# A two-dimensional FFT beside a dense branch: spectral stage on fused real-complex matrices, weight loads on a second queue

## The chip, the cores and the metric

One core of one Trainium2 chip. The metric is the device time of one execution in microseconds (us). TensorE is called PE in the profile (PEld is its weight load), VectorE DVE, ScalarE ACT, GpSimd POOL, SyncE SP. For one core, the record calls a run "fast" when it is within 1.5% of the fastest run of the same kernel; that rule matters below, because it removes most runs of one kernel and few of the other.

## The reference

```python
def _A_ref(x, w_r, w_i):                       # x: (1, 2048, 512), w_r and w_i: (2048, 257)
    X = rfft2(x.astype(float32))
    X = X * (w_r + 1j * w_i)
    return irfft2(X, s=(2048, 512)).astype(bfloat16)

def _B_ref(x, w1, b1, w2):                     # 512 -> 1792 -> 512
    h = x @ w1 + b1
    sp = log1p(exp(-abs(h))) + where(h > 0, h, 0)
    return (h * tanh(sp)) @ w2

g = sigmoid((x * gate_w).sum(-1, keepdims=True))
return g * _A_ref(x, ...) + (1 - g) * _B_ref(x, ...)
```

Everything is bf16 on input. The two branches share only x and the last line, so their matmuls can be mixed freely.

## The kernel before

A Python list scheduler gives every engine a fixed order. It knows an assumed duration and a priority of each task, and it takes, among the tasks that could start within a tolerance of the earliest one, the one of highest priority:

```python
        EPS = 0.25          # tolerance
        SYNC_LAT = 0.25     # assumed latency from engine to engine
        ...
                if est <= best_est + EPS:
                    ...
                    elif (t.prio, t.bl, -t.idx) > (best[1].prio, best[1].bl, -best[1].idx):
                        best = (est, t)
```

The FFT is done by matmuls. Along the rows: `a1`, 16 matmuls of 256 columns for each of 16 row tiles, on half of the array's columns each (`ps<-fdgd,xT` in the profile), then a first stage along the sequence, `s1`. Its results go to a staging buffer of two halves, `T2` (also called `Y1s`; `T` in the profile). From there they are written to DRAM and read back in another order:

```python
            def f_e2(e, t=t, sbank=sbank):        # on ACT or DVE
                return e.activation(Y1s[(t // 4) % 2][:, (t % 4)::4, :], ps[:, sbank, :]..., AF.Copy)
            ...
            if t % 4 == 3:                        # after every fourth tile: two writes of 256 KB
                gi = t // 4
                for bx in range(2):
                    b0 = 16 * bx + 4 * gi
                    t_r1w.append(dma(f"r1w{gi}_{bx}", scr1_w[:, b0:b0 + 4, :], Y1s[gi % 2][:, 4 * bx:4 * bx + 4, :], ...))
```

The third group of four tiles therefore waits until the writes of the first have landed. After the read-back comes the stage that the change rewrites. Its real and imaginary parts lie on separate columns, so that a complex product takes four matmuls each way and an addition:

```python
            def f_s2(e, g=g, xbank=xbank):                      # PE, 4 x 256 columns
                px = ps[:, xbank, :].rearrange("p (c k) -> p c k", c=2)
                e.matmul(px[:, 0, :], CC, In2[:, g, 0, :], start=True, stop=False)
                e.matmul(px[:, 0, :], nSS, In2[:, g, 1, :], start=False, stop=True)
                e.matmul(px[:, 1, :], SSm, In2[:, g, 0, :], start=True, stop=False)
                return e.matmul(px[:, 1, :], CC, In2[:, g, 1, :], start=False, stop=True)
            ...   # DVE: Ps = px * Wr
            ...   # DVE: Qs = px (parts swapped) * WiT
            def f_wmz(e, g=g, pi=pi, zi=zi):                    # POOL
                return e.tensor_tensor(out=Zs[zi], in0=Ps[pi], in1=Qs[pi], op=ALU.add)
            ...   # POOL: column 0 of Zs replaced
            ...   # PE: four matmuls of 256 columns on Zs (s2i), then back through DRAM and s1i, a1i
```

The dense branch: `ps<-xT,w_sb` (mm1), evictions to `hsreg`, exp, ln and tanh on ACT, a product on POOL, `ps<-w_sb,hsreg` (mm2).

## Time and profile before

| what | us |
|---|---|
| median of 4 runs given at first | 171.28 (170.35 to 171.88) |
| median of 16 runs, beside the changed kernel | 171.30 (169.11 to 171.92) |
| the profiled run, its span | 171.84, 170.1 |
| PE busy in it | 159.5 |

The prediction shows the busy table, the chain and the groups. Two readings it did not show matter later. The first is the DMA row of the 40 slices (4.25 us each; a digit is the busy share in tenths):

```profile
DMA  5999999140258466000203020494022010101101
```

The loads fill the queue up to slice 7, 30 us. The second is the start of the timeline: start, duration, engine, operation, operands, count, and in brackets what was waited for.

```profile
4.52 1.92 PE L127 MATMUL ps<-fdgd,xT 128*64 128x256 bf16 x16 [0.96 <-DMA fdgd<-c_fd]
...
8.40 1.92 PE L127 MATMUL ps<-fdgd,xT 128*64 128x256 bf16 x16
...
11.64 1.60 PE L127 MATMUL ps<-fdgd,xT 128*64 128x256 bf16 x16
...
15.18 1.06 PE L127 MATMUL ps<-fdgd,xT 128*64 128x256 bf16 x16
```

The same sixteen matmuls take 1.92 us, then 1.60, then 1.06: the engine starts at about half its speed, and in this run it is at full speed only after 12 to 13 us. I read that row too late: it was in the profile before the prediction, which speaks of "some 14 us of start in which the loads pace PE".

### The profile page before, as it was taken

How to read it: one execution, taken by the hardware profiler on the slowest of the kernel's cores; microseconds unless marked ns; L12 is line 12 of the kernel's file. 1: busy time of each engine (PE TensorE's matmuls, PEld its weight loads, DVE VectorE, ACT ScalarE, POOL GpSimd, SP SyncE). 2: the span in 40 equal slices, each digit the busy share in tenths (PEclk: the TensorE clock that was granted, in tenths of full speed). 3: DMA queues.
4: the chain of work that ended last, by engine and by line, in shares of the span. 5: the costliest groups of instructions: out<-in, count | busy, mean ns of one | idle time of the engine just before them, and what ended most of it. 6: DMA issues, size and time to landing. Idle time of an engine off the chain costs nothing.

```text
span 170.1 us, 2886 instructions
## 1 busy us (share of the span) xinstructions
PE 159.5 (94%) x1130; PEld 88.5 (52%) x1130; DVE 99.2 (58%) x170; ACT 119.2 (70%) x89; POOL 91.0 (53%) x93
## 2 busy tenths in 40 slices
PE   1798999999999998999999999999999999999990
PEld 0576754557656334556666655445555554444440
DVE  1125431247875759978885887557787816071533
ACT  3124576789989997999899989999999980300000
POOL 1000009900000698999999999639991099940000
PEclk9999999999999999999999999999999999999999
DMA  5999999140258466000203020494022010101101
GB/s 166 279 400 390 409 384 339 33 123 4 74 175 233 140 210 285 0 0 31 98 10 118 29 94 39 156 303 122 0 86 99 4 66 0 62 17 49 62 0 62
DMA packets 15058, 21.90 MB, mean 129 GB/s; under 512 B 708, under 2 KB 11972, under 8 KB 14276
## 3 DMA queue, kind: packets, MB, share of 16 engines
q1 hardware_dynamic: 15044, 21.71, 37.7%
q8 instruction: 9, 0.15, 0.3%
q14 instruction: 5, 0.04, 0.1%
HBM read 15.41 MB, written 6.29 MB: 128 GB/s over the span
## 4 chain that ended last, share of the span: by engine, by line
PE 82%; DMA 11%; DVE 3%; issue 1%; SPq 1%
PE ps L127 82%; DMA scr<-T 5%; DMA hsreg<-in_A_x_dram 3%; DMA Abuf<-scr 3%; DVE bs L127 2%; DVE xT L127 1%; SPq L127 1%; DVE T L127 0%; SPq L864 0%; DVE hsreg L127 0%
## 5 line engine op out<-in xcount | busy, mean ns | idle before, releaser
L127 POOL TENSOR_TENSOR hsreg<-hsreg,ureg 128x896 bf16<-128x896 bf16 x32 | 59.4, 1879 | 34.3 <-ACT ureg L127 34.3
L127 PE MATMUL ps<-xT,w_sb 128*128 128x512 bf16 x224 | 53.9, 379 | 0.0
L127 PE MATMUL ps<-w_sb,hsreg 128*128 128x512 bf16 x224 | 51.9, 379 | 0.0
L127 ACT ACTIVATE ureg<-ureg 128x3584 bf16<-128x3584 bf16 x16 | 51.0, 3189 | 0.2
L127 PEld LDWEIGHTS ps<-w_sb,hsreg 128*128 128x128 bf16 x224 | 21.5, 98 | 24.6 <-POOL hsreg L127 0.5
L127 PEld LDWEIGHTS ps<-xT,w_sb 128*128 128x128 bf16 x224 | 20.7, 98 | 22.8 <-DVE hsreg L127 2.5
L127 DVE TENSOR_SCALAR hsreg<-ps,b1f 128x512 bf16<-128x512 f32 x31 | 22.9, 748 | 8.8 <-PE ps L127 7.6
L127 ACT ACTIVATE ureg<-hsreg 128x3584 bf16<-128x3584 bf16 x8 | 25.5, 3189 | 0.2
L127 DVE CAST T<-ps 128x512 bf16<-128x512 f32 x22 | 14.9, 689 | 15.5 <-PE ps L127 15.4
L127 DVE TENSOR_SCALAR bs<-ps,omg 128x512 bf16<-128x512 f32 x15 | 11.3, 751 | 21.5 <-PE ps L127 21.5
L127 ACT ACTIVATE hsreg<-ps,b1f 128x512 bf16<-128x512 f32 x25 | 17.1, 685 | 5.6 <-PE ps L127 5.5
L127 POOL TENSOR_SCALAR WiT<-wizp 128x4096 bf16<-128x4096 bf16 x2 | 7.2, 3604 | 24.1 <-DMA wizp<-in_A_w_i_dram 24.1
L127 PE MATMUL ps<-fdgd,xT 128*64 128x256 bf16 x256 | 18.9, 299 | 1.0 <-DMA fdgd<-c_fd 1.0
L127 POOL TENSOR_TENSOR wizp<-wizp 128x512 bf16<-128x512 bf16 x16 | 18.1, 1154 | 0.0
L127 PEld LDWEIGHTS ps<-fdgd,xT 128*64 128x64 bf16 x256 | 14.4, 120 | 5.0 <-issue 2.9
L127 PE MATMUL ps<-fdgd,TT 128*128 128x512 bf16 x64 | 15.6, 379 | 0.0
L127 DVE COPY xT<-ps 128x512 bf16<-128x512 bf16 x14 | 5.8, 423 | 14.7 <-PE ps L127 14.7
L127 ACT ACTIVATE Abuf<-ps 128x512 bf16<-128x512 f32 x9 | 5.4, 597 | 12.4 <-PE ps L127 12.4
L127 DVE SCALAR_TENSOR_TENSOR bs<-ps,gcol,bs 128x512 bf16<-128x512 f32 x16 | 12.0, 749 | 0.7 <-PE ps L127 0.3
L127 ACT ACT_TABLE_LOAD x9 | 11.5, 1283 | 0.9 <-PEq L929 0.8
L127 DVE TENSOR_TENSOR wizp<-ps,Wr_sb 128x512 bf16<-128x512 f32 x16 | 10.9, 684 | 0.4 <-PE ps L127 0.2
L127 DVE CAST TT<-ps 128x256 bf16<-128x256 f32 x24 | 9.0, 441 | 3.7 <-PE ps L127 3.7
(53 smaller groups left out, 107.3 us busy)
## 6 DMA issues: line engine op xcount, KB each, us to landing
w_sb<-in_B_w_dram SPq DMA_DIRECT2D x4, 896.0 KB, 14.6
scr<-T SPq DMA_DIRECT2D x8, 256.0 KB, 5.5
Abuf<-scr SPq DMA_DIRECT2D x2, 1024.0 KB, 6.2
scr<-T SPq DMA_DIRECT2D x4, 512.0 KB, 2.6
Abuf<-scr SPq DMA_DIRECT2D x4, 512.0 KB, 6.0
out_dram<-bs SPq DMA_DIRECT2D x8, 256.0 KB, 2.0
hsreg<-in_A_x_dram SPq DMA_DIRECT2D x3, 512.0 KB, 7.7
Wr_sb<-in_A_w_r_dram SPq DMA_DIRECT2D x1, 1028.0 KB, 15.1
```

The source lines that it names most:

```text
L127: return f(*a, **kw)
```

## The change

The intent is to put real and imaginary parts both on partitions, so that one 128x128 matrix does the whole complex rotation on 512 columns. The two products with the weights need not be added: two matrices sum them in PSUM. For that the weights must lie twice on the partitions, so they are loaded twice, on a second queue, issued from POOL. The diff cut to its core (`...` marks cuts):

```diff
 def _q_of(c, e):
-    return 32 * (e // 16) + 2 * (e % 16) + c
+    return 64 * c + e
...
-    small = np.stack([np.eye(128), CC, SS, -SS, P0, P1], axis=1)
+    small = np.stack([RF, RI1, RI2, P0k, P1k, Jm], axis=1)
...
+SCH = dict(eps=0.1, sync=0.1)
...
-        EPS = 0.25
-        SYNC_LAT = 0.25
+        EPS = SCH['eps']
+        SYNC_LAT = SCH['sync']
...
+NWARM = 0
+KN = dict(mm1c0=97.0, mm1c=94.0, mish=88.0, mul=89.0, mm2=70.0, bev=94.0, sp0=95.0, gate=96.5)
...
-        t_wr = dma("ld_wr", Wr_sb[:], Wrv, writes=["Wr"], nbytes=128 * 8224)
-        t_wi = dma("ld_wi", Wi_sb, Wiv, writes=["wizp"], nbytes=128 * 8224)
+        t_wr = dma("ld_wr", WaT..., Wrv, writes=["WaT"], nbytes=128 * 16448, queue="pool", deps=t_w1)
+        t_wi = dma("ld_wi", WbT..., Wiv, writes=["WbT"], nbytes=128 * 16448, queue="pool", deps=t_w1)
...          # the two loads of the second dense weights:
-                            writes=[("w2", h)], nbytes=128 * 7 * 1024, ndesc=896))
+                            writes=[("w2", h)], nbytes=128 * 7 * 1024, ndesc=896, queue="pool", deps=t_w1))
...
-        G.cur_prio = 75.0
+        G.cur_prio = KN['gate']
...          # making the negated copy of the imaginary weights (wit) removed; in its place
+        G.add("wb_sgn", "pool", ..., lambda e: e.tensor_scalar(out=WbT[:, :, :], in0=WbT[:, :, :], scalar1=sgnf[:, 0:1], ...))
...          # inside the loop of 16 steps:
-                px = ps[:, xbank, :].rearrange("p (c k) -> p c k", c=2)
-                e.matmul(px[:, 0, :], CC, In2[:, g, 0, :], start=True, stop=False)
-                ...three more
+                return e.matmul(ps[:, xbank, :], RFm, In2ck[:, 2 * gp:2 * gp + 2, :]..., start=True, stop=True)
...
-                return e.tensor_tensor(out=Zs[zi], in0=Ps[pi], in1=Qs[pi], op=ALU.add)
...
-                e.matmul(pt[:, 0, :], CC, Zs[zi][:, 0, :], start=True, stop=False)
-                ...three more
+                e.matmul(ps[:, tbank, :], RI1m, P1s[pi]..., start=True, stop=False)
+                return e.matmul(ps[:, tbank, :], RI2m, P2s[pi]..., start=False, stop=True)
```

The correction of column zero is rewritten to the new layout, with one more tiny matmul (`Jm`), and two scalings of the gate move from DVE to ACT. `NWARM` is a set of warm-up matmuls that is coded but switched off.

> **What bounds the kernel now.** I read the page first: the busy table, then the chain that ended last, because a busy engine only matters if the chain runs over it.
>
> ```profile
> PE 159.5 (94%) x1130; PEld 88.5 (52%) x1130; DVE 99.2 (58%) x170; ACT 119.2 (70%) x89; POOL 91.0 (53%) x93
> ...
> PE 82%; DMA 11%; DVE 3%; issue 1%; SPq 1%
> ```
>
> The tensor engine is 94% busy and carries 82% of the chain. Next, the same chain in order of time, for where it leaves the tensor engine.
>
> ```profile
> 17.09 32.44 PE ps L127 x304
> ...
> 51.41 8.48 DMA scr<-T
> ...
> 60.03 4.91 DMA Abuf<-scr
> 64.95 0.05 issue
> 64.99 99.49 PE ps L127 x576
> 164.48 0.02 issue
> ```
>
> The reader should see two things. From 64.99 to 164.48 us the chain is one unbroken stretch of matmuls. And the excursion through DRAM (51.4 to 65 us), although the chain names it, costs the engine nearly nothing. The table of waits and the busy times by stretch say so:
>
> ```profile
> PE ps L127 <- DMA Abuf<-scr: 0.7, 1, 0.7
> ...
> 2.96:17.09 14.13, 11.56 (x118) 8.64 (x119) 4.54 (x13) 3.58 (x6) 0.00 (x0) 1.00 0.99 353
> 17.09:65.00 47.91, 46.98 (x430) 26.09 (x430) 26.02 (x41) 41.35 (x34) 16.65 (x17) 1.00 0.60 199
> 65.00:104.00 39.00, 39.00 (x250) 23.98 (x251) 32.26 (x55) 36.21 (x29) 38.87 (x53) 1.00 0.15 59
> ```
>
> PE idles 0.7 us for the read-back, and 47.91 - 46.98 = 0.93 us in all from 17.09 to 65; the matmuls of the dense branch fill the rest. From 65 to 104 us, where the changed stage lies, PE is busy all 39.00 us. POOL is then busy 38.87 us, so there are two full engines in that stretch, and I must decide which one sets the pace. PE has no gap at all, so POOL does not make it wait. So the time is: 3.0 us until the first matmul, some 14 us of start in which the loads pace PE, 149 us of full PE, and a tail of about 4.1 us (two evictions and the last store after the last matmul ends at 165.97).
>
> The engine's real price is not the busy column. The matmul rows show 379 ns for one of 512 columns, but that is latency; they overlap. From the timeline a run of 28 takes 6.21 us, so the spacing is (6.21 - 0.379) / 27 = 0.216 us. A run of eight with 256 columns takes 1.04 us: (1.04 - 0.273) / 7 = 0.110 us.
>
> ```profile
> 145.74 6.21 PE L127 MATMUL ps<-w_sb,hsreg 128*128 128x512 bf16 x28
> ...
> 71.89 1.04 PE L127 MATMUL ps<-Abuf,sm 128*128 128x256 bf16 x8
> ```
>
> The groups concerned, with the shapes kept apart:
>
> ```profile
> L127 POOL TENSOR_TENSOR wizp<-wizp 128x512 bf16<-128x512 bf16 x16 | 18.1, 1154 | 0.0
> ...
> L127 PE MATMUL ps<-Abuf,sm 128*128 128x256 bf16 x64 | 9.0, 273 | 0.7 <-DMA Abuf<-scr 0.7
> L127 PE MATMUL ps<-wizp,sm 128*128 128x256 bf16 x64 | 8.5, 273 | 0.0
> ...
> L127 POOL TENSOR_SCALAR WiT<-wizp 128x4096 bf16<-128x4096 bf16 x2 | 7.2, 3604 | 24.1 <-DMA wizp<-in_A_w_i_dram 24.1
> ```
>
> Their busy times (9.0 and 8.5) contain overlap with neighbours of other groups at each change, so I price them by spacing: 64 x 0.110 = 7.0 us each.
>
> **What the Trainium skill says.** "TensorE: Matmul & The Clock Gate", section "Back-to-back issue gap", gives N / 2.4 + 2.5 ns for a warm array: 216 ns at 512 columns, 109 at 256. The trace agrees (0.216 and 0.110). The same section also names 131 ns per matmul at 512 for a sustained stream; this trace does not show that. The consequence is that cost goes by columns: one matmul of 512 columns saves almost nothing over two of 256, only fewer total columns do. "DMA: Bandwidth & Descriptors", section "Issuing engines are not separate DMA queues", says that transfers started by different engines still run on the same 16 DMA engines, so a second queue saves issue time[...], not bandwidth. Nothing in this trace tests it, since all data transfers are issued from SP; but the page shows DMA full (nines) only in the first seven slices. The same page, section "SWDGE vs HWDGE vs iDMA", says that GpSimd computes the descriptors itself and that the engines take turns between the two kinds of queue; no row here has a duration for that.
>
> **The change, part by part.**
>
> 1. Forward second stage. Before: 16 steps of four 256-column matmuls (real and imaginary parts on separate columns), 1024 columns a step. After: real and imaginary parts both lie on partitions, the whole complex rotation is one 128x128 matrix, one 512-column matmul a step. Cost: 64 x 0.110 = 7.0 us becomes 16 x 0.216 = 3.5 us. Saved: 3.5 us, all of it on PE in the full stretch.
>
> 2. Inverse second stage. Before: four of 256 columns a step, after the multiply and add. After: two of 512, since the two products go to PSUM unadded and two matrices sum them. Cost: 7.0 us becomes 32 x 0.216 = 6.9 us. Saved: 0.1 us. The gain goes to POOL instead.
>
> 3. POOL. The 16 additions leave: 18.1 us. Making the negated and copied imaginary weights (7.2 us) leaves, and the sign multiply over 8224 columns takes its place. At 3604 / 4096 = 0.88 ns a column that is an estimated 7.2 us, so nothing is won there. 16 small column patches stay. POOL loses about 18 us net, beside PE, and by the stretch above PE did not wait for it: 0 us on the path. Its value is that the products of the dense branch, which shared POOL with the additions (products and additions alternate from 65 to 102 us), come earlier. That gives the scheduler more matmuls to choose from.
>
> 4. DVE. Two products a step over 512 columns before and after (16 x 0.684 + 16 x 0.682 = 21.8 us): unchanged.
>
> 5. Weights. Both spectral weight tensors are read twice into duplicated partitions: 1.03 MB each becomes 2.1 MB, so 2.1 MB more. At the 390 to 400 GB/s of the full slices that is an estimated 5.3 us more of DMA. These loads now start from POOL after the dense first weights have landed, so roughly from 20 to 38 us with the second dense weights behind them (6 MB at 400 GB/s is 15 us). They are needed at 65 us (spectral) and 58 us (second dense layer): hidden.
>
> 6. The correction of column zero: four tiny matmuls become one, one swap matmul is added. I put -0.1 us on PE. Its chain gains one hop over PE and one over DVE. Two DVE scalings of the gate move to ACT: nothing.
>
> 7. The schedule. The order on every engine comes from a list scheduler. Its tolerance goes from 0.25 to 0.1 us, its assumed latency between engines also from 0.25 to 0.1, and the gate's matmuls move earlier. That removes no work. The small gaps inside full PE: after 17.09 us I count 146.3 us of matmuls by spacing in 147.9 us, so 1.6 us of them exist to be won. But a shorter assumed latency is optimistic: a matmul's result comes 379 - 216 = 163 ns after its slot is over, so a consumer placed 0.1 us later is placed too early. Taken together I book zero, with an uncertainty of 1 us either way.
>
> Sum on the path: 3.5 + 0.1 + 0.1 = 3.7 us, with perhaps 0.3 us from a shortened 0.7 us wait and a smoother tail. 171.28 - 4.0 = 167.3 us, a ratio of 0.977.
>
> **Rivals.**
>
> ACT becomes the bound. It is busy 35.26 of 35.5 us from 104 to 139.5 us, so it paces the dense branch. But its last large activation ends at 139.51 us, the last POOL product at 150.66; with one half group (7 x 0.216 = 1.5 us) and the tail of 4.1 us this limit is 156.3 us against a span of 170.1. A saving of 4 us does not reach it. If it did, the time would stay above 169.
>
> The new two-deep buffer stalls PE. The summed spectra had four buffers; the new products have two, and a step cannot go on until the inverse matmuls two steps before are done. These wait for the column-zero chain, with its two extra hops and POOL's products of 1.88 us in its way. PE issues in order, so a step placed too early holds everything behind it. Before, column zero was ready at about 75 us, ten after the read-back, and PE filled the time with other matmuls. For the rival: the optimistic latency of part 7. Against it: plenty of dense matmuls are left at that moment, and POOL is freer. I give it a loss of 0.5 to 2 us if it comes, so 168 to 169.5.
>
> The second queue disturbs the forward spectra. The writes to DRAM from 22 to 50 us, formerly behind the weights in one queue, now take turns with 6 MB of loads. If the two staging buffers fill, PE stops in order. It would cost 1 to 3 us, and 169 to 170. Against it: each staging buffer has over 10 us before it is needed again. It could even help, as the writes no longer stand behind weights.
>
> The reordering gains more than the matrices. If the scheduler recovers the micro gaps (1.6 us), part of the start and some of the tail, the time is 164 to 165.5.
>
> **Range and chances.** The removed columns are the certain part. The rest is roughly symmetric with a spread of about 2 us: 164.8 to 169.8 holds it 8 times in 10. The 2% line lies at 171.28 x 0.98 = 167.85, only half a microsecond above my number, so the chance of faster is only moderately above one half: 0.58. Slower needs a real stall of over 7 us somewhere, 0.04; the rest is 0.38.
>
> **What would show it right or wrong.** Right: the forward matmuls appear as 16 of 512 columns and the inverse as 32, PE has about 4 us less busy time, it is still 94% busy, POOL's busy time is some 18 us lower, and no new PE wait exceeds 1 us. DVE within 1 us of 99. Wrong in part 1: PE's busy time falls by 4 us and the span does not; then a new wait should stand between 20 and 50 us (staging, second queue) or between 65 and 105 us (column zero, two buffers). Wrong in part 7: the span falls by clearly more than PE's busy time, with the difference in the first 17 us or after the last matmul. Wrong in part 5: a wait for the weight loads ahead of the first spectral product, or the second dense layer starting well after 58.5 us.

## The result, and the profile after

| | median us | lowest to highest | runs |
|---|---|---|---|
| before | 171.30 | 169.11 to 171.92 | 16 |
| after | 169.49 | 166.61 to 171.30 | 11 |

The ratio of the fast runs is 0.9816, with an interval from 0.975 to 0.9883: the 2% line lies inside it, so the verdict is unclear. This ratio, and each below, is the mean time of one kernel's fast runs over that of the other's of the same rounds, so not quite the ratio of the medians quoted. Here the difference is large. Only 3 of the 11 runs after (166.61, 168.03, 168.16) are within 1.5% of the fastest, but 11 of the 16 before. Over all runs the means are 169.31 and 171.09, a ratio of 0.990. (The record's list of states has a twelfth run of after, 169.11 us, which its count leaves out; it would not change the reading.) So the first thing to explain is not a time but a spread: 4.7 us after, against 2.8 before.

The profile of after is of its fastest run (166.61 us), that of before is of one of its slower (171.84). A comparison of the two flatters the change: the spans differ by 5.3 us, the medians by 1.8. With that in mind, the page of after:

```profile
PE 155.6 (94%) x1047; PEld 77.8 (47%) x1047; DVE 100.5 (61%) x170; ACT 118.0 (72%) x90; POOL 78.0 (47%) x79
...
DMA  5999389994445859000030303038801113010101
...
PE 91%; DVE 3%; DMA 3%; issue 1%; SPq 0%
```

PE is 94% busy as before, with 3.9 us less of it, and the chain is PE even more than before. The DMA row has a dip in its fifth slice (a slice is 4.12 us here), and the loads then go on to the ninth, about 37 us. That is the second queue: its loads wait for the first dense weights to land. The groups of the new stage, and the stretches of the middle:

```profile
L144 PE MATMUL ps<-Abuf,sm 128*128 128x512 bf16 x16 | 4.9, 379 | 0.0
...
L144 PE MATMUL ps<-bs,sm 128*128 128x512 bf16 x32 | 8.4, 379 | 0.0
...
L144 POOL TENSOR_SCALAR WbT<-WbT,sgnf 128x8224 bf16<-128x8224 bf16 x1 | 7.1, 7118 | 0.1
```

```profile
15.64:53.60 37.96, 37.81 (x374) 21.03 (x374) 20.91 (x34) 31.02 (x30) 14.59 (x21) 1.00 0.68 241
53.60:104.00 50.40, 50.36 (x232) 21.44 (x233) 41.02 (x67) 48.45 (x30) 32.94 (x35) 1.00 0.28 102
```

The matmul counts are those of the diff, 16 and 32 of 512 columns. PE (first pair of each row) is busy 37.81 of 37.96 us and 50.36 of 50.40: nothing in the new stage makes it wait. POOL, which was full from 65 to 104 us, is now busy 32.94 of 50.4.

To separate the 5.3 us, I priced each matmul of both traces by its slot: columns / 2.4 ns + 2.5 ns (the formula of the prediction), the half-array `a1` ones 62 ns each, the tiny ones 27 ns (64 of the gate take 1.74 us). Together they come to 153.0 us before and 149.3 after, 3.7 less. The tail, from the last matmul's end to the span's end, is 4.14 and 4.11 us. The rest is the start, where after is ahead by 1.45 us and has done one more `a1` group, 1.0 us:

```profile
4.76 1.92 PE L144 MATMUL ps<-fdgd,xT 128*64 128x256 bf16 x16 [1.16 <-DMA fdgd<-c_fd]
...
8.04 1.21 PE L144 MATMUL ps<-fdgd,xT 128*64 128x256 bf16 x16
...
9.96 1.07 PE L144 MATMUL ps<-fdgd,xT 128*64 128x256 bf16 x16
```

Here the engine is almost at full speed in the second group and at full speed from the third; before, in its slower run, from the fourth. Against that, the time after the start (from 17.09 us before, 15.64 after) that no slot explains grew from 2.6 to 3.5 us, 0.85 more. Most of that is one row:

```profile
20.48 13.01 PE L144 MATMUL ps<-xT,w_sb 128*128 128x512 bf16 x56
```

(13.01 - 0.379) / 55 = 0.230 us a matmul where 0.216 would do. The new schedule issues the first chunk of the dense branch in one piece, and its two PSUM banks are emptied by DVE or ACT in between: weight loads waiting for an eviction by DVE rose from 2.5 to 8.2 us. The sum, 3.7 + 1.45 + 1.0 + 0.03 - 0.85 = 5.3 us, is what was to be explained, and 2.4 of it are the start.

The theories that I took to the experiments are three. **The matrices** take 3.7 us off, whatever else happens. **The start** at half speed differs from run to run and makes both kernels' times spread. **The second queue** (called theory C in some of the expectations) holds up the first write of the staging buffer in some runs of the changed kernel and stops PE; the rival is that the changed kernel's slow runs are nothing but slow starts.

On the start the Trainium skill has this: "TensorE: Matmul & The Clock Gate", section "What's actually happening", says that the array's clock is halved by default, that about 3.4 us of activity in a free-running window releases it, and that the moment therefore varies from run to run. The traces agree: 1.92 us against 1.06 for the same work. Their records of the granted clock, which the views do not list, begin with the release: at 8.39 us in after, 12.78 in before. (For the time ahead of that the views print 1.00 for want of a record, so the durations are the evidence there.)

### The profile page after: what moved, and what is told of

Its sections match the earlier page's. It is cut to its first block, busy times and chain, and to the rows that moved or that the text cites. A ratio compares the mean times of both kernels' runs of the same rounds, so it can differ in the third digit from the quotient of the medians.

```text
span 164.8 us, 2686 instructions
## 1 busy us (share of the span) xinstructions
PE 155.6 (94%) x1047; PEld 77.8 (47%) x1047; DVE 100.5 (61%) x170; ACT 118.0 (72%) x90; POOL 78.0 (47%) x79
## 4 chain that ended last, share of the span: by engine, by line
PE 91%; DVE 3%; DMA 3%; issue 1%; SPq 0%
PE ps L144 91%; DMA hsreg<-in_A_x_dram 3%; DVE bs L144 2%; DVE xT L144 1%; SPq L144 0%; DVE hsreg L144 0%; DVE T L144 0%
## 5 line engine op out<-in xcount | busy, mean ns | idle before, releaser
L144 DVE TENSOR_SCALAR hsreg<-ps,b1f 128x512 bf16<-128x512 f32 x37 | 27.7, 750 | 14.6 <-PE ps L144 13.4
L144 PEld LDWEIGHTS ps<-xT,w_sb 128*128 128x128 bf16 x224 | 19.1, 97 | 30.0 <-DVE hsreg L144 8.2
L144 PE MATMUL ps<-fdgd,xT 128*64 128x256 bf16 x256 | 17.9, 286 | 1.2 <-DMA fdgd<-c_fd 1.2
L144 DVE CAST T<-ps 128x512 bf16<-128x512 f32 x19 | 12.8, 687 | 6.6 <-PE ps L144 6.4
L144 PEld LDWEIGHTS ps<-fdgd,xT 128*64 128x64 bf16 x256 | 13.6, 114 | 4.1 <-DVE xT L144 1.8
L144 ACT ACTIVATE hsreg<-ps,b1f 128x512 bf16<-128x512 f32 x19 | 13.0, 684 | 3.4 <-PE ps L144 3.2
L144 DVE TENSOR_TENSOR bs<-ps,WaT 128x512 bf16<-128x512 f32 x16 | 10.3, 684 | 0.3 <-PE ps L144 0.3
L144 DVE TENSOR_TENSOR bs<-ps,WbT 128x512 bf16<-128x512 f32 x16 | 10.2, 682 | 0.0
L144 DVE CAST TT<-ps 128x256 bf16<-128x256 f32 x22 | 8.1, 438 | 3.0 <-PE ps L144 3.0
L144 POOL DMA_DIRECT2D WaT<-in_A_w_r_dram x1 | 0.8, 803 | 19.0 <-DMA w_sb<-in_B_w_dram 19.0
```

The costliest lines, as they stand in the source:

```text
L144: return f(*a, **kw)
```

## The experiments

Three sets of runs, on three chips; kernels of one set ran on the same chip and are compared there. "Warm" below means that a few matmuls on zeros are put ahead of the first work and between the first two pieces of it, so that the clock is released earlier (in the two profiles of experiment 2, at 5.27 us before and 6.93 after).

### 1. The changed kernel again, nothing edited

> The changed kernel once more, unedited, for a second profile. The first profiled run (166.61 us) was the fastest of 11, the kernel before was profiled in one of its slower runs (171.84). Theory A (the tensor engine's start at half clock lasts differently long from run to run): in a run near the median of 169.5 us, the first groups of 16 forward matmuls take about 1.9 us instead of 1.06 for longer than in the first profile (where only the first did), and the stretch after 17 us is as long as in the first profile within 0.3 us. Rival B (a wait in the middle that comes and goes, from the second queue or the two buffers): the start is as in the first profile and a new wait of the tensor engine of 1 to 3 us stands after 17 us.

Median 166.96 us of 8 runs (166.37 to 170.92), before on the same chip 170.26 of 43 (169.08 to 172.69), ratio 0.9803 (0.9756 to 0.9849). Six runs lie between 166.37 and 168.70, and two are at 169.45 and 170.92. By luck the profiled run is the one of 169.45, 2.8 us slower than the profiled run of after. Theory A expected no longer stretch after 17 us and rival B no slower start; each is half right, for its start shows one slow group more (the clock is released at 10.44 us):

```profile
7.98 1.92 PE L144 MATMUL ps<-fdgd,xT 128*64 128x256 bf16 x16
...
10.87 1.06 PE L144 MATMUL ps<-fdgd,xT 128*64 128x256 bf16 x16
```

And later it has this, in the order of time, from its timeline:

```profile
20.57 0.80 POOL L144 DMA_DIRECT2D WaT<-in_A_w_r_dram  x1 [19.18 <-DMA w_sb<-in_B_w_dram]
...
21.29 0.92 SPq L144 DMA_DIRECT2D scr<-T  x2
...
41.43 0.60 ACT L144 ACTIVATE T<-ps 128x512 bf16<-128x512 f32 x1 [2.57 <-DMA scr<-T]
...
42.17 0.38 PE L144 MATMUL ps<-Abuf,m1g 128*128 128x256 bf16 x2 [2.00 <-ACT T L144]
```

The same lines of the fastest run (after):

```profile
20.36 0.80 POOL L144 DMA_DIRECT2D WaT<-in_A_w_r_dram  x1 [18.98 <-DMA w_sb<-in_B_w_dram]
...
20.38 0.92 SPq L144 DMA_DIRECT2D scr<-T  x2
...
38.55 0.60 ACT L144 ACTIVATE T<-ps 128x512 bf16<-128x512 f32 x1 [0.60 <-DMA scr<-T]
```

Read them from the bottom. The eviction into staging waits until the first pair of writes has left the buffer. In the fast run that costs ACT 0.60 us and PE nothing. In the slow run the pair was issued 0.91 us later, after POOL's first load instead of level with it. The two writes of the pair have to be told apart here. In the fast run the first landed 2.2 us after its issue and only the second was held up, for 17.7 us, to 38.44. In the slow run both were, for 17.0 and 19.6 us, and the second landed at 41.32 (the median of the twelve writes is 2.6 us in both runs). ACT then waits 2.57 us and PE 2.00. So the slow run has both causes at once: some 0.9 us from the start, 2.0 from the staging buffer. The two are linked: a slow start delays the write, while the loads are tied to the landing of the first dense weights and don't move with it.

Both queues share the engines. In the fast run between 18 and 46 us:

```profile
q0 software_dynamic: 768, 6.05, 56.3%
q1 hardware_dynamic: 2139, 1.08, 12.8%
```

The columns are packets, MB, and the share of the engines. POOL's queue moves packets of 7.9 KB on average, 16,448 B for the spectral weights; the writes are packets of 0.5 KB.

### 2. Both kernels warm

```diff
-NWARM = 0
+NWARM = 4                     # four 512-column matmuls on zeros before the first transposes
...
+            if t == 0:          # and two more after the first tile's transposes
+                G.add("warm2", "pe", 2 * 0.43, f_warm2, reads=["wreg", ("x", 0)], writes=[("bank", 1)], deps=[t_tr[0]], prio=99.5)
```

The same lines were put into the kernel before.

> The changed kernel with four matmuls on zeros before the first transposes and two after them, so that the engine is busy while it waits for the first loads; the order of everything else is the same. Theory A: the clock is released before the bulk of the transposes in every run, the spread of the runs shrinks from 4.7 us to under 1.5 us, and the median falls to 165.5 to 167 us. Rival B: the median stays at 169 to 170 and the spread stays.

> The kernel before with the same six matmuls on zeros, order otherwise the same. Theory A: the same gain at the start, median 169 to 170.5 us, and the difference to the changed kernel with the warm start is the removed matmul columns, 3.7 us (3 to 4.5). If the schedule's constants gained or lost something of their own, the difference is under 3 or over 4.5 us.

| same chip | median us | lowest to highest | runs | ratio to before (interval) |
|---|---|---|---|---|
| before, warm | 169.61 | 168.88 to 170.38 | 22 | 0.9969 (0.995 to 0.9988) |
| after, warm | 166.04 | 165.84 to 167.01 | 6 | 0.9774 (0.9733 to 0.9814) |

The start of after, warm:

```profile
1.39 1.89 PE L144 MATMUL ps<-hsreg 128*128 128x512 bf16 x4 [1.39 <-POOL hsreg L144]
...
3.50 1.06 PE L144 MATMUL ps<-hsreg 128*128 128x512 bf16 x2
4.69 1.92 PE L144 MATMUL ps<-fdgd,xT 128*64 128x256 bf16 x16
...
7.65 1.07 PE L144 MATMUL ps<-fdgd,xT 128*64 128x256 bf16 x16 [0.29 <-DVE xT L144]
```

Only one group is slow, and the spread falls from 4.6 to 1.2 us (before: from 3.6 to 1.5). The medians differ by 169.61 - 166.04 = 3.57 us; the prediction's sum for the matrices and the column-zero correction is 3.7. This pair compares the two kernels with the start nearly alike. It is not matrices alone: in the profiles of the two, the time after the start that no slot explains is 2.4 us before and 3.3 after, 0.9 more, and the new order's start is ahead again, with one more `a1` group done, by 0.2 us in this pair and by 1.0 in the profile of experiment 3. So the schedule's loss and gain nearly cancel, and part of the agreement is that cancelling. The warm-up itself wins 0.65 us of the median in before and 0.92 in after.

### 3. The second forward stage twice

```diff
+                e.matmul(ps[:, xbank, :], RFm, In2ck[:, 2 * gp:2 * gp + 2, :]..., start=True, stop=True)
                 return e.matmul(ps[:, xbank, :], RFm, In2ck[:, 2 * gp:2 * gp + 2, :]..., start=True, stop=True)
```

> The changed kernel with the warm start, and each of the 16 forward second-stage matmuls issued twice (the second overwrites the first, the result is unchanged, the order and the durations the scheduler sees are unchanged). If the tensor engine is the bound throughout that stage, this costs 16 x 0.216 = 3.5 us over the warm changed kernel. If the stage has slack of its own (column zero, two buffers, POOL), it costs under 2 us.

169.56 us (169.18 to 170.33, 22 runs), 3.52 above after, warm, on the same chip. The sixteen added matmuls at 0.216 us come to 3.46. Put back what the forward matrices took away and the whole gain is gone: 169.56 against the 169.61 of before, warm. This shows that the stage lies on the path, matmul by matmul; that the gain is in the columns taken out follows from it and the sum.

### 4. The second dense weights only after the first writes

```diff
-            t_w2.append(dma(f"ld_w2_{h}", ..., queue="pool", deps=t_w1))
...
+                if gi == 0:            # right behind the first two writes
+                    for h in range(2):
+                        t_w2.append(dma(f"ld_w2_{h}", ..., queue="pool", deps=list(t_r1w), prio=99.0))
```

> The changed kernel (cold start) whose second-layer weight loads, last on POOL's queue, wait until the first two writes of the forward spectra to DRAM have landed; every engine's order is the same. Theory C (POOL's loads hold back the first spectra writes, issued at 20.4 to 21.3 us, until POOL's queue is drained at 38 to 41 us; the staging buffer is then freed late and the tensor engine waits up to 2 us): the queue drains 4 us earlier, the writes land by 35 us instead of 38 to 41, no run has the 2 us wait, and the runs above 168.3 us vanish: median 166.3 to 167.2, spread under 2 us. Rival A alone (only the half-clock start differs between runs): the spread and the share of runs at 168.5 to 171 stay as they were.

Not warm. 167.97 us (166.73 to 169.07, 6 runs; before on that chip 169.90 of 11), ratio 0.9871 (0.9821 to 0.9921). The median misses what was expected, and two runs lie above 168.3 us. The profiled run (167.91) has a slow start and no PE wait for staging. Its two writes, issued from 21.66 us, both behind the first load, landed only at 36.45 and 37.20 us, not by 35: the spectral weights alone, 4.1 MB, held them up for some 15 us. Still, set beside the slow run of experiment 1, whose writes were both behind the loads too, the pair is free 4.1 us earlier (37.20 against 41.32). The profile speaks for theory C, the times do not decide: none is above 169.07, but six are few. Inconclusive.

### 5. All weights on the first queue

```diff
         order = G.schedule()
+        mv = [t for t in order["pool"] if t.isdma]      # the four loads go to SP, ahead of the first write
+        for t in mv:
+            order["pool"].remove(t)
+            t.deps = []
+            t.eng = "sp"
+        i_ = [t.name[:3] for t in order["sp"]].index("r1w")
+        order["sp"][i_:i_] = mv
```

> The changed kernel (cold start) with its four POOL loads issued from SP right behind the first-layer weights instead, as before the change; every other engine's order is the same. So there is no second queue and the data engines have no pause between 17 and 22 us. Theory C: in one queue the writes stand behind all loads but these end earlier, so they land before 35 us and no tensor wait arises: median 166.3 to 167.2 and no runs at 169 to 171, that is, the second queue gained nothing and cost the slow runs. Rival (the second queue helps, as the change intends): slower than the changed kernel by over 1 us.

Not warm: 167.30 us (166.05 to 168.85, 6 runs), ratio 0.9806 (0.9756 to 0.9857). That is 0.1 us above what theory C expected, with no runs at 169 to 171, and not the loss of over 1 us of the rival: the unedited kernel had 0.9803 in experiment 1.

> The warm changed kernel with its four POOL loads issued from SP right behind the first-layer weights, order of the other engines the same. If the second queue is worth nothing for the time: median 165.7 to 166.3, beside 166.0. If it is worth something: 167 or more.

Warm, on the third chip: 166.43 us (166.06 to 166.59, 6 runs; before there 170.38 of 27), ratio 0.976 (0.9719 to 0.9801). Neither profile shows an ACT or PE wait for staging. The spread of the warm one, 0.5 us, is the smallest of all kernels here. Its median lies just above the band for "worth nothing", and its ratio equals that of after, warm (0.9774) within the intervals. So the second queue wins nothing that these runs can tell, and in the two profiles without it PE has no wait for the write. After warm, with either queue, has lower medians than both kernels as they stand.

A by-product: POOL is busy 75.1 us in it, against 78.4 in after, warm. The four issues cost POOL 3.3 us of its own time.

### 6. More bytes on the second queue

```diff
+                e.dma_start(w2_sb[:, 7 * h:7 * (h + 1), :], w2v[...]).then_inc(t.sem, 16)
+                return e.dma_start(bs[:, 6 * h:6 * h + 6, :], w2v[:, 7 * h:7 * h + 6, :])   # a second copy, 1.6 MB in all, not used
```

> The warm changed kernel with 1.6 MB of extra loads (copies of the second-layer weights into idle buffers) on POOL's queue; order the same, result the same. Theory C: POOL's queue drains about 4 us later (near 42 us), the first writes land with it, and the tensor engine waits 3 to 4.5 us for the staging buffer: median 169 to 170.5 us against 166.0. Rival D (all transfers simply share the bandwidth; the writes are 0.5 MB and need little): the writes land as before, the loads are hidden, median 166 to 166.5.

166.16 us (165.76 to 166.69, 4 runs), ratio 0.9772 (0.9715 to 0.9828). What the second-queue theory expected failed: nothing happened. In the profiled run the pair was issued from 19.74 us, 0.36 ahead of the first load; the first write landed at 22.59 and the second, 17.0 us after its issue, at 37.12. So it is not the amount at the end of the loads' queue that matters. My reading, argued and not shown by this run alone, is that a write issued ahead of the loads is through before they come.

The landings of the single writes go further. A write has 32 packets for each of the 16 engines; the loads of the changed kernel have 44, first 16 of 16,448 B, then 28 of 4096 B. Suppose that one packet of a write goes for one of the loads. Then one write that stands against the loads is done with their 32nd packet, and what is loaded behind that does not matter. Worked out from the landings of the loads, this estimate gives 38.5 us for the second write of after (measured 38.44), 38.4 for the first of the slow run (38.32), and 36.7 here (37.12). Two writes against the loads, 64 packets, outlast the 44: in the slow run the second landed at 41.32, the loads at 40.85. It is not exact: in the profile of experiment 3 the second write landed at 32.5 already. The decisive quantity would then be the order of issue. That asked for a run which forces the other order.

### 7. The first write forced behind the loads

```diff
+                        def f_late(e, t_=t_, f0=t_.fn):       # five transfers of 8 KB ahead of the first write
+                            for i in range(5):
+                                e.dma_start(scr2[i, 0:16, :], d_FD[0:16, 0, 0:256]).then_inc(t_.sem, 16)
+                            return f0(e)
```

> The warm changed kernel with five tiny transfers put in front of the first write of the forward spectra on SP, which delays that write by about 2 us, to 22.6 us, behind POOL's weight loads in every run. Theory C, amended (the two queues take turns packet by packet; a write issued after the loads waits its many turns behind their 16 KB packets, one issued a microsecond ahead of them does not): it lands at 40 us or later, ACT waits 2 to 4 us for it, the tensor engine 1.5 to 3.5 us, median 167.5 to 169.5. Rival: a write delayed by 2 us has over 10 us of slack, median 166.0 to 166.5.

172.08 us (171.59 to 173.21, 4 runs), ratio 1.0104 (1.0044 to 1.0163): one per cent slower than the kernel before, through the delay of one pair of writes. The direction was as expected, the size far above it. The five issues take SP from 20.24 to 23.69 us, longer than the 2 us meant, POOL's loads start at 21.03, and both writes of the pair are held up: they land at 39.66 and 41.84 us, the loads at 41.25. (The five themselves stand before it with 5 packets of 512 B an engine, which this run does not tell apart from the order.) Then:

```profile
42.69 0.54 PE L144 MATMUL ps<-Abuf,m1g 128*128 128x256 bf16 x2 [3.57 <-ACT T L144]
43.16 3.40 PE L144 MATMUL ps<-fdgd,xT 128*64 128x256 bf16 x32
```

and of the windows, the stretch after the wait (its third number from the right is PE's clock):

```profile
42.60:46.50 3.90, 3.81 (x35) 2.80 (x35) 1.39 (x2) 3.89 (x2) 2.09 (x3) 0.56 0.07 21
```

PE stands for 3.57 us, which is the wait of experiment 1 made longer. That is not all: the mean clock of this stretch is 0.56 (the trace's record has it at half from 42.78 to 46.19 us), and the next 32 `a1` matmuls take 3.40 us where they took 1.94 in the fastest run. 3.57 + 1.46 = 5.0 us of the 5.3 above the warm kernel with the scheduler's former constants (166.82 us, next experiment), on the same chip. A wait long enough makes PE pay twice. The section of the skill named above says so too: after an idle window of about 3.4 us the clock is halved again. The trace agrees, with 3.57 us idle; in experiment 1, with 2.00 us idle, the clock record stays at 1.0.

### 8. The scheduler's constants and the gate's priority

```diff
-SCH = dict(eps=0.1, sync=0.1)
+SCH = dict(eps=0.25, sync=0.25)
-KN = dict(..., gate=96.5)
+KN = dict(..., gate=75.0)
```

> The warm changed kernel with the scheduler's former constants (tolerance 0.25, latency 0.25, gate late); matrices and queues as changed. The prediction booked zero for the constants, with 1 us either way: median 165.5 to 167, beside 166.0 with the new constants. If the constants carry part of the gain, it is 167.5 or more; if the optimistic latency costs something, under 165.5.

197.53 us (196.67 to 197.97, 6 runs), ratio 1.1599. Where I had expected next to nothing, 31 us. The table of waits, then the timeline:

```profile
PE ps L144 <- ACT gth L144: 26.5, 1, 26.5
```

```profile
98.82 6.41 ACT L144 ACTIVATE ureg<-ureg 128x3584 bf16<-128x3584 bf16 x2
...
105.13 0.17 ACT L144 ACTIVATE gth<-ps 128x16 f32<-128x16 f32 x1
105.36 0.29 PE L144 MATMUL ps<-wrev,sm 128*128 128x128 bf16 x2 [26.48 <-ACT gth L144]
```

The tiny matmuls of the column-zero weights write the same PSUM bank as the gate's. With the gate's tasks at low priority, its tanh stands behind a whole chunk of large activations on ACT, and since PE issues in order, everything stops for 26.5 us. The rest of the 31 I have not divided; in part it is the clock, which the trace has at half until 111.63 us. Which of the edits did it? Only the two constants put back, the gate left early:

```diff
-SCH = dict(eps=0.1, sync=0.1)
+SCH = dict(eps=0.25, sync=0.25)
```

> The warm changed kernel with tolerance and latency of the scheduler back at 0.25 us but the gate still early. With all three constants back it took 197.5 us, and the tensor engine waited 26.5 us in one place, for the gate's tanh on ACT, which lay behind the activations of a whole chunk. If the gate's priority alone carries that: no such wait here, and the two other constants are worth what the prediction booked, zero within 1 us: median 165.0 to 167.0. If the tolerance or latency carries it: over 175 us.

166.82 us (166.38 to 167.13, 6 runs), ratio 0.9786 (0.9744 to 0.9828); after, warm, has 0.9774. The constants are worth nothing that these runs can tell, and the gate's place carries the 31 us. It is no gain of the change, since the kernel before had the low priority and no such wait; it is a condition of the change.

### 9. POOL's additions in the kernel before

```diff
-                return e.tensor_tensor(out=Zs[zi], in0=Ps[pi], in1=Qs[pi], op=ALU.add)
+                return e.tensor_tensor(out=Zs[zi][:, :, 0:2], in0=Ps[pi][:, :, 0:2], in1=Qs[pi][:, :, 0:2], op=ALU.add)
```

On the kernel before, warm. The result is wrong on purpose (relative error 0.048): only the cost is asked for.

> The warm kernel before with its 16 additions on POOL cut to two columns each (wrong result on purpose, same order on every engine): POOL loses about 15 us of work, nothing else changes. The prediction: POOL's additions lie beside the tensor engine and are worth 0 us: median 169.3 to 169.9, beside 169.6. If POOL paced that stage: 167 or less.

169.38 us (168.77 to 173.65, 22 runs), ratio 0.9944 (0.9926 to 0.9962), against 0.9969 (0.995 to 0.9988) for before, warm, on another chip.

```profile
PE 158.8 (95%) x1119; PEld 87.5 (52%) x1136; DVE 98.8 (59%) x170; ACT 119.2 (71%) x89; POOL 76.8 (46%) x94
```

POOL went from 91.5 us busy (before, warm) to 76.8, and the time by some 0.25%, 0.4 us, with intervals that overlap. (One run, 173.65, is slow and not in the ratio.) An engine that was 38.87 of 39.00 us busy in that stretch gave up its work and nobody noticed.

## Why the prediction was right or wrong

The number, 167.3 us (164.8 to 169.8), holds the median of 169.49 near its upper end, and the repeat's median, 166.96, close to its middle. By the steps:

1. **Forward stage, 3.5 us: right.** Doubling it cost 3.52 us. **Inverse stage and column zero, 0.1 + 0.1: right as far as the sum can tell:** the warm pair differs by 3.57 where the sum is 3.7, and the slots of the matmuls by 3.67. In the warm pair the schedule's loss and gain have to cancel for that (experiment 2).
2. **POOL, "about 18 us net" and 0 on the path.** The path part is right (0 to 0.4 us, experiment 9). The size is off: 91.0 to 78.0 is 13 us. The term missed is the new work: the four load issues take 3.3 us of POOL's time, which I had not counted as work at all, and the remaining 1.7, by difference, is added copies and clearings of weight columns and wider steps of column zero. The sign multiply itself is as estimated, 7.1 us for 7.2.
3. **DVE unchanged: nearly.** 99.2 to 100.5, a little over the 1 us that I allowed.
4. **Weights "hidden": right for their use, wrong for their company.** They arrived long before they were needed. But the third rival, which I put down with "each staging buffer has over 10 us before it is needed again", is what happens in part of the runs. That is the step that failed. The time until reuse is about 17 us (from 21.3 to 38.5), and I set no landing time against it; in the trace of before, behind the weights in one queue, this pair had taken 9.3 and 8.6 us. A write behind the loads takes 16 to 20 us, so the margin is zero: the fast profile waits 0.6 us on ACT and nothing on PE, the slow one 2.0 us on PE, the forced one 3.57. Its size, "1 to 3 us, and 169 to 170", is what the profiled slow run shows (2.0 us; 169.45).
5. **Zero for the schedule: right for the constants, blind for the gate.** The prediction lists the gate's move among the things that remove no work. True; without it the new schedule has a stall of 26.5 us.
6. **The rival "two-deep buffer": did not come.** PE is busy 50.36 of 50.40 us over the whole stage.
7. **The rival "ACT becomes the bound": did not come.** The last stretch has the tail it had before, 4.11 us for 4.14.
8. **The rival "reordering gains more": no.** The micro gaps grew by 0.85 us. There were also more of them to win than the prediction says: it subtracts 146.3 from 147.9, but 165.97 - 17.09 is 148.9, so they were 2.6 us and not 1.6. The start is no evidence for it either: what the profiles show in the first 17 us is in large part the clock's luck. The prediction took a difference "in the first 17 us or after the last matmul" as evidence on the schedule; it was evidence on the start, which differs by 0.9 us between two runs of one kernel.

What remains open: which of the runs of 169 to 171 us in the first result suffered from the staging wait and which only from the start. One slow run of the changed kernel was profiled, and it had both. Nor is it settled how the engines share out turns. The skill ("DMA: Bandwidth & Descriptors", section "Queues, rings and completion order") has each engine go round the queues packet by packet. Counting packet for packet, as in experiment 6, puts the end of the slow pair just behind the end of the loads (44 load packets an engine, 64 of the pair), and it landed there, 41.32 against 40.85 us. In experiment 4 only 16 load packets stood against the 64, and the pair again landed behind them, 37.20 against 35.94; my 35 us had not been counted that way. But no run was made to test the count, and one profile departs from it.

The difference of the medians, 1.8 us in the first runs and 3.3 in the repeat, is therefore some 3.6 us of matrices, with a schedule that about breaks even, less what late writes and slow starts give back in part of the runs. That last share is argued from two profiled runs and the forced one; the share of each in a median was not measured.

## What to carry to other kernels

Where one engine is the path almost without gaps, price a change by that engine's slots, and then ask only two more questions: what does the new order of transfers do to a buffer that is nearly late already, and which tiny task now stands behind a large one in an in-order queue. Moving loads to a second queue doesn't put them out of the way of small writes on the first; check how long such a write takes with the loads running, not alone. When the spread of the runs is as large as the effect, make the start alike in both kernels before comparing, and look at which runs a filter drops.

## What the Trainium skill lacked or had wrong

- "DMA: Bandwidth & Descriptors", section "Issuing engines are not separate DMA queues", says that a second issuer doesn't bring bandwidth. It lacks the price for the other queue: a write of 256 KB in packets of 512 B, issued behind loads in packets of 4 to 16 KB on POOL's queue, took 16.0 to 19.6 us to land in the profiles of experiments 1 and 7, where the median is 2.6.
- The same page, section "Queues, rings and completion order", says that each engine goes round the queues with work, packet by packet. Taking the profile's packets for the page's, the landings fit one for one: the slow pair at 41.32 us (the loads' end at 40.85), the second write of the fast run at 38.44 (38.5 by the count), the pair with the second dense weights held back at 37.20 (the loads' end at 35.94). One profile departs from it (experiment 6).
- The same page, section "SWDGE vs HWDGE vs iDMA", gives packets of 4096 B as preferred on GpSimd's path; the trace shows 256 packets of 16,448 B there. No page gives the busy time that an issue costs GpSimd: 0.67 to 1.1 us each here, 3.3 us for four.
- "TensorE: Matmul & The Clock Gate", section "What's actually happening", puts the penalty of the ramp below 1% of a kernel. The warm-up here won 0.65 and 0.92 us of the medians of 170, which agrees; but it cut the spread from 3.6 to 1.5 us and from 4.6 to 1.2. That a wait in mid-kernel brings the half clock back is on the page; the price of a single one here: after 3.57 us of idling the next 32 matmuls took 1.46 us longer.
- The same page, section "Back-to-back issue gap", names 131 ns per matmul of 512 columns for sustained streams; no run here shows it. The longest streams run at 216 ns, or 230 where PSUM banks were emptied late.
